# Block means of the first group issued from ScalarE, smaller pieces of v, and other places for q, w_val and k loads in a fused attention and gated-convolution kernel

## The chip, the cores and the metric

The kernel runs on one core of one Trainium2 chip. The metric is device time in microseconds (us); three runs of the kernel before gave a median of 293.86 us (293.66 to 294.35). PE is TensorE, DVE is VectorE, ACT is ScalarE, POOL is GpSimd, and SP is SyncE, which here only issues DMAs. PEld is the loading of weights into PE.

## The reference

Attention over 4 batches and 8 heads of 768 positions, 64 wide, in which each query sees a window of its neighbours and one summary of every block of 32 positions, followed by a projection, a causal convolution that makes a gate, and a second projection:

```python
k_sum = k.reshape(B, H, nb, block, D).max(axis=3)      # block 32: maximum of k
v_sum = v.reshape(B, H, nb, block, D).mean(axis=3)     # mean of v
mask_l = np.abs(pos[:, None] - pos[None, :]) < window  # window 16
scores_all = np.concatenate([scores_l_m, scores_s + log(block)], axis=-1)
a = softmax(scores_all)
x = a @ np.concatenate([v, v_sum], axis=2)             # (4, 768, 512) after a transpose
gate = sigmoid(causal_conv5(x, conv_w))
out = (gate * (x @ w_val)) @ w_out
```

All inputs are float32 except those that the kernel takes as 64-bit words and converts on the chip (w_val, w_out and the convolution weights).

## The kernel before

**Units and groups.** A unit is one pair of heads over four tiles of 64 queries; there are 48, numbered u = 0 to 47. Four units (the four pairs `pr`) make a group g = u // 4, a third of a batch. For each unit, `stage_s` multiplies q by a tile of 120 columns of k per query tile (window, own block of 64, and the 24 block maxima), DVE masks the scores and finds row minima (`sn`, `nm`), ACT takes the exponent (`p`), `stage_n` normalises on POOL, `stage_t` transposes on PE and copies to SBUF on ACT (`pt`, `pts`), and `stage_av` multiplies by v (`x`), copies the result out on ACT (`xf`, `xh`), splits it on POOL (`xl`) and makes the five convolution taps on ACT or DVE (`g`). When a group's four units are through, eight pieces of projection work are queued for PE: `val` (four, with w_val) and `out` (two, with w_out).

**Data in SBUF.** `qbd` has two buffers, one per group in turn. Each pair has two buffers of k, one per batch in turn. v has two buffers, one per group in turn: `v_g` takes the place of `v_(g-2)`, and its load has to wait until the last unit of that group (u = 4(g-2) + 3) has been multiplied. A v buffer holds, on 120 partitions, 16 rows before the tile, 64 own rows, 16 rows after, and twice 12 rows of block means. The three groups of loaded rows come by three DMAs (`load_v`, L110, of 8192 bytes a row), and the 24 rows of means by four DMAs from the small tile `vs` in SBUF (`fill_vs`, L166). In k, `prep_k` (L117) computes the block maxima (`ks`) on DVE and copies them between the loaded columns; only then can a unit of the new batch use that k. For the means of v, `prep_v` adds on POOL, or in batch 0 `prep_v0` on DVE, from a transposed copy `vT`.

**What sets the order.** SP's instructions stand in the order of the code. The other engines' orders are made by a scheduler when the kernel is built, from the same code. `LOADS` (L44) is the order of the first loads: k, q, vT of batch 0 (n), mask (m), identity (i), v of group 0, convolution weights (c), the four rows of w_val (w), and q of group 1 (Q). After them `side_work` (L451) runs once per step s (step s issues `stage_s` of unit s and `stage_av` of unit s - 4): at s = 3 it places the means of groups 0 and 1 and loads v of group 1, at s = 5 it loads w_out, at the first pair of each later group it loads the next q, at the last pair it loads the next v and places its means. `LOAD_K` and `PREP_K` (L47, L48) give, per pair, the step of a batch at which the next batch's k and vT are loaded, and at which they are prepared (first row for the first batch, second row for the others).

**Semaphores of the DMAs.** Each DMA, from whichever engine, reports its landing on one of eight semaphores, DMAHW0 to DMAHW7, taken in turn. A DMA waits on its issuing engine until the DMA eight places earlier, which had the same semaphore, has landed.

Of the kernel before, what the change touches and what calls it, by code (L numbers as in the profile page):

```python
# [17 lines left out]
B, H, S, D = 4, 8, 768, 64  # L18
DM = H * D
BLK, WIN = 32, 16  # L20
NB = S // BLK
QT = 64
NT = S // QT
NPR = H // 2
NTH = 3
TPU = NT // NTH
# [9 lines left out]
KALLOC = OFF_A + 2 * STEP * (NT // 2 + 1)  # L36
NK = 5
HALO = NK - 1
REBIAS = 2.0 ** ((127 - 1023) // 8)
LAG_N, LAG_T, LAG_AV = 1, 3, 4  # L40
PROJ_RATE = 1.015
VAL_COST, OUT_COST = 1.32, 2.6
ACT_TAP_G = 5
LOADS = "k0 q0 m k1 q1 n0 i k2 q2 n1 k3 q3 n2 n3 v0 c w0 w1 Q w2 w3"  # L44
CONVERT = {"wv": (0, 0, 1, 0), "wo": (6, 9, 6, 11)}
SPLIT = {"wv": (12, 4, 10, 5), "wo": (12, 9, 12, 12)}
LOAD_K = ((6, 7, 8, 9), (1, 2, 8, 4))  # L47
PREP_K = ((9, 10, 11, 11), (5, 8, 9, 8))  # L48
PREP_V0 = (1, 2, 3, 3)


# [1 line left out]
def tile_attention_then_gated_conv(  # L53
# [13 lines left out]
    nc = tc.nc  # L67
# [13 lines left out]
    for i in range(NQB):  # L81
        t = cpool.tile([P, NPR, SG], F32, tag=f"qbd{i}", name=f"qbd{i}")
# [13 lines left out]
    def load_q(g):  # L96
        b, th = divmod(g, NTH)
        nc.sync.dma_start(qbd[g % NQB], qT[b, th])

    def load_k(b, pr):  # L100
        t = ld.tile([P, KALLOC], F32, tag=f"k{pr}", name=f"k_{b}_{pr}")
        nc.sync.dma_start(t[:, :KTOT], kT[b, pr])
        ktile[b, pr] = t

    def load_vT(b, pr):
        t = ld.tile([P, S], F32, tag="vT", name=f"vT_{b}_{pr}")
        nc.sync.dma_start(t, vT[b, pr])
        vTt[b, pr] = t

    def load_v(g):  # L110
        b, th = divmod(g, NTH)
        t = ld.tile([KW, TPU, DM], F32, tag="v", name=f"v_{g}")
        for r0, r1, s0 in ((0, WIN, 0), (OFF_O, OFF_B, WIN), (OFF_N, KW, WIN + QT)):
            nc.sync.dma_start(t[r0:r1], vw[b, th, s0 : s0 + r1 - r0])  # L114
        vtile[g] = t

    def prep_k(b, pr):  # L117
        t = ktile[b, pr]
        ks = wk.tile([P, NB], F32, tag="ks", name=f"ks_{b}_{pr}")
        own = t[:, OFF_O : OFF_O + STEP * NT].rearrange("p (t c) -> p t c", c=STEP)[:, :, :QT]  # L120
        nc.vector.tensor_reduce(  # L121
            ks.rearrange("p (t j) -> p t j", j=2),
            own.rearrange("p t (j c) -> p t j c", c=BLK),
            AX.X,
            ALU.max,
        )
        for half, n in ((0, NT // 2 + 1), (1, NT // 2)):
            c0 = OFF_A + half * STEP
            dst = t[:, c0 : c0 + 2 * STEP * n].rearrange("p (t c) -> p t c", c=2 * STEP)[:, :, :HB]
            src = ks[:, half * HB : half * HB + HB]  # L130
            nc.vector.tensor_copy(dst, src.unsqueeze(1).broadcast_to([P, n, HB]))  # L131
# [32 lines left out]
        vsum[b] = t  # L164

    def fill_vs(g):  # L166
        b = g // NTH
        src = vsum[b]
        vr = vtile[g].rearrange("p (t e) c -> p e t c", e=2)
        for e in range(2):  # L170
            for half in range(2):
                off = OFF_A if (e == half) else OFF_B
                nc.sync.dma_start(  # L173
                    vr[off : off + HB, e],
                    src[half * HB : half * HB + HB].unsqueeze(1).broadcast_to([HB, TPU // 2, DM]),
                )
# [5 lines left out]
    def to_f32(dst, raw, n, nm, bufs):  # L182
        words = raw.rearrange("p (n two) -> p two n", two=2)
        low, high = words[:, 0], words[:, 1]
        sc = wk.tile([P, n], F32, tag=f"sc{n}", name=f"sc_{nm}", bufs=bufs)
        nc.scalar.activation(sc, high.bitcast(F32), AF.Copy, scale=REBIAS)
        hi = sc.bitcast(U32)
# [43 lines left out]
    def load_cw():  # L231
        dst = cwt.rearrange("p a k -> p (a k)")
        if not wide:
            nc.sync.dma_start(dst, cw)
            return
        raw = cpool.tile([P, 2 * NPR * NK], U32, tag="cwraw", name="cwraw")
        nc.sync.dma_start(raw, cw.bitcast(U32))
        to_f32(dst, raw, NPR * NK, "cw", 1)

    def load_w4(nm, src, ks):  # L240
# [6 lines left out]
        n=load_vT0,  # L247
        w=lambda i: load_w4("wv", wv, (i,)),
        v=load_v,
        m=lambda i: nc.sync.dma_start(mask, maskc),  # L250
        i=lambda i: nc.sync.dma_start(ident, identc),
        c=lambda i: load_cw(),
        Q=lambda i: load_q(1),
    )
    for a in LOADS.split():
        acts[a[0]](int(a[1]) if len(a) > 1 else 0)
# [6 lines left out]
    def group(g):  # L263
        if g not in grp:
# [3 lines left out]
                gt=wk.tile([P, NPR, SG], F32, tag="gt", name=f"gt_{g}"),  # L268
                xf=wk.tile([P, NPR, HALO + SG], F32, tag="xf", name=f"xf_{g}"),
            )  # L270
            halo = grp[g]["xf"][:, :, :HALO]
            if g % NTH == 0:
# [69 lines left out]
    def stage_av(u):  # L342
# [16 lines left out]
        x = G["xf"]  # L359
        c0 = HALO  # L360
        if g:
# [20 lines left out]
    def proj_val(g, co):  # L382
# [5 lines left out]
        if g == 0:  # L388
            for ci in range(4):
                nc.tensor.matmul(  # L390
                    pp[:, :SG], wvf[:, ci, cs], G["xf"][:, ci, HALO:],
                    start=(ci == 0), stop=(ci == 3),
# [62 lines left out]
    def side_work(s):  # L455
# [8 lines left out]
        if s == NPR - 1:  # L464
            prep_vs(0)
            fill_vs(0)
            load_v(1)
            fill_vs(1)
        if s == NPR + 1:
            load_w4("wo", wo, (2, 3, 0, 1))  # L470
        if s >= NPR and g + 1 < NG:
            if pr == 0:
                load_q(g + 1)
            if pr == NPR - 1:
                load_v(g + 1)
                if th + 1 < NTH:
                    fill_vs(g + 1)
        if b + 1 < B:
            for i in range(NPR):
                if w == LOAD_K[b > 0][i]:  # L480
                    load_k(b + 1, i)
                    load_vT(b + 1, i)
                if w == PREP_K[b > 0][i]:
                    prep_k(b + 1, i)
# [38 lines left out]
def _layout(q, k, v, moe_w_val, moe_conv_w, moe_w_out):  # L523
    f = np.float32
    qT = q.reshape(B, NPR, 2, NTH, SG, D).transpose(0, 3, 2, 5, 1, 4)
    qT = qT.reshape(B, NTH, 2 * D, NPR, SG)
    kt = k.reshape(B, NPR, 2, S, D).transpose(0, 1, 2, 4, 3).reshape(B, NPR, 2 * D, S)
    kT = np.zeros((B, NPR, 2 * D, KTOT), f)
    for t in range(NT):
        c = OFF_O + STEP * t  # L530
        kT[..., c : c + QT] = kt[..., t * QT : (t + 1) * QT]
    vT = v.reshape(B, NPR, 2, S, D).transpose(0, 1, 2, 4, 3).reshape(B, NPR, 2 * D, S)
    vn = np.zeros((B, S + 2 * WIN, DM), f)
    vn[:, WIN : WIN + S] = v.transpose(0, 2, 1, 3).reshape(B, S, DM)
    vw = np.zeros((B, NTH, QT + 2 * WIN, TPU, DM), f)
    for t in range(NT):
        vw[:, t // TPU, :, t % TPU] = vn[:, t * QT : t * QT + QT + 2 * WIN]
    cw = moe_conv_w.reshape(NK, NPR, 2 * D).transpose(2, 1, 0).reshape(2 * D, NPR * NK)

    def words(a):  # L540
        a = np.ascontiguousarray(a)
        return a.view(np.int64) if a.dtype == np.float64 else a

    loc = np.full(KW, -1)
    loc[:WIN] = np.arange(WIN)
    loc[OFF_O:OFF_B] = WIN + np.arange(QT)
    loc[OFF_N:] = WIN + QT + np.arange(WIN)
    qi = np.arange(2 * D)[:, None] % QT
    second = np.arange(2 * D)[:, None] >= QT
    maskc = np.zeros((2 * D, 3, KW), f)  # L550
    for mv in range(3):
        lo = np.where((mv == 0) & ~second, WIN, 0)
        hi = np.where((mv == 2) & second, WIN + QT, QT + 2 * WIN)
        ok = (loc > qi) & (loc < qi + 2 * WIN) & (loc >= lo) & (loc < hi)
        m = np.where(ok, 0.0, -1.0e9 * math.sqrt(D))
        m = np.where(loc[None, :] < 0, math.log(BLK) * math.sqrt(D), m)
        maskc[:, mv] = m
    return dict(
        qT=qT, kT=kT, vT=vT, vw=vw, wv=words(moe_w_val), cw=words(cw), wo=words(moe_w_out),
        maskc=maskc, identc=np.eye(2 * D, dtype=f),  # L560
    )
# [24 lines left out]
```

## Time and profile before

| | us |
|---|---|
| median of three runs | 293.86 |
| profiled execution, whole time | 295.11 |
| its span, first to last instruction | 293.3 |
| PE busy | 250.3 |
| DVE busy | 218.0 |
| ACT busy | 190.1 |
| POOL busy | 155.0 |

The profile's page gives the busy time per engine, then the span in 40 slices of 7.33 us with the busy share of each in tenths, then the chain of work that ended last. The other views are answers drawn from the same trace: the timeline (start, duration, engine, line, operation, out<-in, and in brackets the idle time of the engine before it and what ended it), the waits (engine and line, whom it waited for: total us, times, longest), windows (a stretch, its length, busy time of PE, PEld, DVE, ACT and POOL with counts, then granted PE clock, DMA share and GB/s), and groups of instructions (count, busy us, mean ns of one, idle before). SPq rows of a timeline show when SP issued a DMA and how long the issue took, not the transfer. The profiled execution lies 1.25 us above the median of the runs shown.

### The profile page before, as it was taken

To read this page: it belongs to the slowest core of one execution; us is meant where nothing else is said; L and a number is where in the kernel's file an instruction comes from. 1 tells how busy PE (TensorE), PEld (TensorE's weight loads), DVE (VectorE), ACT (ScalarE), POOL (GpSimd) and SP (SyncE) were. 2 spreads that over 40 slices of the span, in tenths; PEclk is the share of its full clock that TensorE was granted. 3 is DMA by queue.
4 is the path that set the end of the run, shared out by engine and by line. 5 is a ranking of instruction groups with operands and counts; after the bars stand their busy time and mean duration, and the time that the engine had idled before them with its cause. 6 is when DMAs were issued, how large, how long until landed. Compare 5 with 4: busy or idle time off the path is not lost.

```text
span 293.3 us, 7550 instructions
## 1 busy us (share of the span) xinstructions
PE 250.3 (85%) x2592; PEld 200.8 (68%) x2592; DVE 218.0 (74%) x827; ACT 190.1 (65%) x686; POOL 155.0 (53%) x224
## 2 busy tenths in 40 slices
PE   1352856999989998979989889699999999999994
PEld 0231634677767775867766677589888887989893
DVE  1948789988679857756749988587898897876420
ACT  1436868857966975947955978377695877735231
POOL 0124346998677666455467578264465453723240
PEclk9999995599999999999999999979999999999999
DMA  7999690781484283660474476706335052202011
GB/s 221 385 242 303 177 368 4 211 305 55 111 254 160 70 207 125 165 200 3 116 235 169 133 235 172 230 0 160 123 104 141 2 152 93 75 0 75 0 74 72
DMA packets 15302, 43.46 MB, mean 148 GB/s; under 512 B 2592, under 2 KB 3360, under 8 KB 14112
## 3 DMA queue, kind: packets, MB, share of 16 engines
q1 hardware_dynamic: 15264, 42.98, 47.7%
q8 instruction: 21, 0.34, 0.5%
q14 instruction: 17, 0.14, 0.2%
HBM read 34.32 MB, written 6.29 MB: 138 GB/s over the span
## 4 chain that ended last, share of the span: by engine, by line
PE 43%; DMA 22%; SPq 13%; DVE 10%; ACT 7%; issue 2%; ACTq 0%
PE val L397 15%; PE out L419 13%; DMA k<-in_kT_dram 12%; SPq L173 7%; PE x L351 7%; PE s L293 4%; PE pt L337 4%; DMA v<-in_vw_dram 3%; DMA v<-vs 3%; SPq L114 3%; DVE g L377 3%; DMA qbd<-in_qT_dram 3%; ACT p L316 3%; DVE ks L121 2%; DVE k L131 2%
## 5 line engine op out<-in xcount | busy, mean ns | idle before, releaser
L377 DVE SCALAR_TENSOR_TENSOR g<-xf,cwt,g 128x256 f32<-128x256 f32 x192 | 93.2, 486 | 7.2 <-ACT g L370 3.7
L316 ACT ACTIVATE p<-sn,nm 128x120 f32<-128x120 f32 x192 | 74.1, 391 | 27.4 <-DVE nm L305 24.3
L397 PE MATMUL val<-xh,wv 128*128 128x256 f32 x352 | 75.2, 296 | 2.2 <-ACT xh L362 1.2
L328 POOL TENSOR_TENSOR p<-p,ri 128x480 f32<-128x480 f32 x48 | 48.5, 1011 | 33.1 <-DVE ri L326 20.9
L397 PEld LDWEIGHTS val<-xh,wv 128*128 128x128 f32 x352 | 57.6, 192 | 6.2 <-ACT xh L362 2.6
L419 PE MATMUL out<-wo,gh 128*128 128x512 f32 x192 | 60.8, 402 | 1.1 <-ACT ob L425 1.1
L365 POOL TENSOR_TENSOR xl<-xf,xh 128x256 fp32r<-128x256 f32 x44 | 32.4, 737 | 41.0 <-ACT xf L363 40.9
L397 PE MATMUL val<-xl,wv 128*128 128x256 f32 x176 | 50.6, 290 | 0.0
L293 PE MATMUL s<-k,qbd 64*64 64x120 f32 x768 | 37.8, 300 | 14.9 <-DVE nm L305 6.1
L407 POOL TENSOR_TENSOR gl<-gf,gh 128x256 fp32r<-128x256 f32 x48 | 35.0, 734 | 22.6 <-ACT gh L406 22.2
L305 DVE CUSTOM_DVE_ANT_0 sn<-s,mask 128x120 f32<-128x120 f32 x192 | 43.7, 275 | 4.2 <-PE s L293 3.9
L293 PEld LDWEIGHTS s<-k,qbd 64*64 64x64 f32 x768 | 23.9, 146 | 26.4 <-issue 11.8
L351 PE MATMUL x<-pts,v 120*64 120x64 f32 x768 | 34.4, 232 | 7.5 <-DMA v<-vs 3.5
L419 PEld LDWEIGHTS out<-wo,gh 128*128 128x128 f32 x192 | 34.2, 188 | 8.4 <-ACT ob L425 1.5
L351 PEld LDWEIGHTS x<-pts,v 120*64 120x64 f32 x768 | 27.3, 140 | 18.1 <-issue 4.6
L337 PE MATMUL pt<-ident,p 128*120 128x128 f32 x192 | 33.3, 299 | 5.3 <-ACT pts L339 3.9
L316 ACT ACTIVATION_READ_ACCUMULATOR p<-sn,nm 128x1 f32 x192 | 37.2, 194 | 0.0
L419 PE MATMUL out<-wo,gl 128*128 128x512 f32 x96 | 37.1, 400 | 0.0
L142 POOL TENSOR_TENSOR vT<-vT 128x384 f32<-128x384 f32 (+3 forms) x48 | 27.4, 577 | 18.1 <-DMA vT<-in_vT_dram 16.7
L397 PEld LDWEIGHTS val<-xl,wv 128*128 128x128 f32 x176 | 33.8, 192 | 1.0 <-issue 0.5
L380 ACT ACTIVATE gt<-g 128x256 f32<-128x256 f32 x48 | 18.7, 389 | 22.4 <-DVE g L377 22.1
L405 DVE SCALAR_TENSOR_TENSOR gf<-gt,val 128x256 f32<-128x256 f32 x48 | 19.7, 417 | 15.3 <-PE val L397 13.1
(44 smaller groups left out, 300.8 us busy)
## 6 DMA issues: line engine op xcount, KB each, us to landing
k<-in_kT_dram SPq DMA_DIRECT2D x16, 478.0 KB
vT<-in_vT_dram SPq DMA_DIRECT2D x16, 384.0 KB
v<-in_vw_dram SPq DMA_DIRECT2D x12, 512.0 KB
out_dram<-ob SPq DMA_DIRECT2D x24, 256.0 KB
qbd<-in_qT_dram SPq DMA_DIRECT2D x11, 512.0 KB
v<-in_vw_dram SPq DMA_DIRECT2D x24, 128.0 KB
v<-vs SPq DMA_DIRECT2D x48, 48.0 KB
raw_wv<-in_wv_dram SPq DMA_DIRECT2D x4, 512.0 KB
```

The lines of the kernel that those rows point to most:

```text
L142: nc.gpsimd.tensor_tensor(dst, src[:, :, :n], src[:, :, n : 2 * n], ALU.add)
L293: nc.tensor.matmul(sp[64 * e : 64 * e + 64, h, j * KW : j * KW + KW], qbd[g % NQB][64 * h : 64 * h + 64, pr, i * QT : i * QT + QT], ktile[ ...
L305: nc.vector.tensor_tensor_reduce(sn[:, n, :], sp[:, h, j * KW : j * KW + KW], mask[:, mv, :], -1.0 / math.sqrt(D), 3.0e38, ALU.add, ALU.mi ...
L316: nc.scalar.activation(p[:, n, :], sn[:, n, :], AF.Exp, bias=nm[:, n : n + 1], scale=-1.0, accum_out=rs[:, n : n + 1],)
L328: nc.gpsimd.tensor_tensor(pn, s["p"], ri.unsqueeze(2).broadcast_to([P, TPU, KW]), ALU.mult)
L337: nc.tensor.transpose(pt[:KW, i, :], s["pn"][:, i, :], ident)
L351: nc.tensor.matmul(xp[h * D : (h + 1) * D, i * QT : (i + 1) * QT], v[:, i, c0 : c0 + D], s["pts"][:, 2 * (i // 2) + h, (i % 2) * QT : (i % ...
L365: nc.gpsimd.tensor_tensor(G["xl"][:, pr, :], x[:, pr, c0 : c0 + SG], G["xh"][:, pr, :].bitcast(F32), ALU.subtract)
L377: nc.vector.scalar_tensor_tensor(gt, x[:, pr, o : o + SG], cwt[:, pr, k : k + 1], gt, ALU.mult, ALU.add)
L397: nc.tensor.matmul(pp[:, :SG], w[:, ci, cs], G[x][:, ci, :], start=(n == 0), stop=(n == 11))
L407: nc.gpsimd.tensor_tensor(G["gl"][:, co, :], gf, G["gh"][:, co, :].bitcast(F32), ALU.subtract)
L419: nc.tensor.matmul(pp, G[gx][:, ci, si * P : si * P + P], w[:, ci, :], start=(n == 0), stop=(n == 11))
```

## The change

The four DMAs that place the means of group 0 are issued by ACT instead of SP (later groups stay on SP). v lies in DRAM as two halves of two tiles each, so that each row of a v load is two pieces of 4096 bytes instead of one of 8192. In the first loads, the last two rows of w_val come before q of group 1. `LOAD_K` and `PREP_K` have other steps.

```diff
+VP = TPU // 2
-LOADS = "k0 q0 m k1 q1 n0 i k2 q2 n1 k3 q3 n2 n3 v0 c w0 w1 Q w2 w3"
+LOADS = "k0 q0 m k1 q1 n0 i k2 q2 n1 k3 q3 n2 n3 v0 c w0 w1 w2 w3 Q"
-LOAD_K = ((6, 7, 8, 9), (1, 2, 8, 4))
-PREP_K = ((9, 10, 11, 11), (5, 8, 9, 8))
+LOAD_K = ((5, 6, 8, 9), (1, 2, 5, 6))
+PREP_K = ((7, 8, 10, 11), (4, 5, 8, 9))
@@ load_v
-            nc.sync.dma_start(t[r0:r1], vw[b, th, s0 : s0 + r1 - r0])
+            src = vw[b, th, :, s0 : s0 + r1 - r0].rearrange("e r t c -> r e t c")
+            nc.sync.dma_start(t[r0:r1].rearrange("r (e t) c -> r e t c", e=VP), src)
@@ fill_vs
+        eng = nc.sync if g else nc.scalar
-                nc.sync.dma_start(
+                eng.dma_start(
@@ _layout
-    vw = np.zeros((B, NTH, QT + 2 * WIN, TPU, DM), f)
+    vw = np.zeros((B, NTH, VP, QT + 2 * WIN, 2, DM), f)
-        vw[:, t // TPU, :, t % TPU] = vn[:, t * QT : t * QT + QT + 2 * WIN]
+        i = t % TPU
+        vw[:, t // TPU, i // 2, :, i % 2] = vn[:, t * QT : t * QT + QT + 2 * WIN]
```

Three places show what this does to the order of instructions. The first is on ACT, near the start: `vs_0` are the means, `sc_cw` and `sc_wv0..3` the first step of converting the weights, `p_3` the exponents of unit 3, `pts_1` the copy of unit 1's transposed weights. In brackets stands what a row waits for. Before:

```order
L339 COPY pts_0_285<-pt_0_280 120x512 [waits PE_49]
L186 ACTIVATE sc_cw_117<-cwraw_115 128x20 [waits DMAHW1_49]
L186 ACTIVATE sc_wv0_137<-raw_wv0_122 128x512 [waits DMAHW2_49]
L316 ACTIVATE p_3_289,rs_3_291<-sn_3_288,nm_3_290 128x120 [waits DVE_49] x3
L339 COPY pts_1_343<-pt_1_338 120x512 [waits PE_49]
L186 ACTIVATE sc_wv1_142<-raw_wv1_124 128x512 [waits DMAHW3_49]
```

And now:

```order
L342 COPY pts_0_285<-pt_0_280 120x512 [waits PE_49]
L189 ACTIVATE sc_cw_117<-cwraw_115 128x20 [waits DMAHW1_49]
L176 DMA v_0_111<-vs_0_262 12x2x512 [waits DMAHW2_49,Activation_49]
L176 DMA v_0_111<-vs_0_262 12x2x512 [waits DMAHW4_49]
L189 ACTIVATE sc_wv0_137<-raw_wv0_122 128x512
L176 DMA v_0_111<-vs_0_262 12x2x512 [waits DMAHW6_49]
L189 ACTIVATE sc_wv1_142<-raw_wv1_124 128x512 [waits DMAHW3_49]
L176 DMA v_0_111<-vs_0_262 12x2x512 [waits DMAHW0_49]
L319 ACTIVATE p_3_289,rs_3_291<-sn_3_288,nm_3_290 128x120 [waits DVE_49] x4
L342 COPY pts_1_343<-pt_1_338 120x512 [waits PE_49]
```

Four DMAs with waits of their own have moved in ahead of `p_3` and `pts_1`. Counted through the eight semaphores, they wait for the landing of the first row of w_val, of the third, of q of group 1, and of the middle piece of v of group 1.

The second place is on SP, where k of batch 3 is loaded (`k_3_2` is batch 3, pair 2; `v_8` the v of group 8). Before:

```order
L98 DMA qbd0_81<-in_qT_dram 128x1024
L102 DMA k_3_3_2224<-in_kT_dram 128x956
L107 DMA vT_3_3_2226<-in_vT_dram 128x768
L426 DMA out_0_dram<-ob_3_1_2241 128x512
L114 DMA v_8_2474<-in_vw_dram 16x2048
L114 DMA v_8_2474<-in_vw_dram 64x2048
L114 DMA v_8_2474<-in_vw_dram 16x2048
L173 DMA v_8_2474<-vs_2_1823 12x2x512 x4
L98 DMA qbd1_82<-in_qT_dram 128x1024
L102 DMA k_3_2_2564<-in_kT_dram 128x956
```

And now:

```order
L99 DMA qbd0_81<-in_qT_dram 128x1024
L429 DMA out_0_dram<-ob_3_1_2247 128x512
L103 DMA k_3_2_2319<-in_kT_dram 128x956
L108 DMA vT_3_2_2321<-in_vT_dram 128x768
L103 DMA k_3_3_2396<-in_kT_dram 128x956
L108 DMA vT_3_3_2398<-in_vT_dram 128x768
L116 DMA v_8_2488<-in_vw_dram 16x2x1024
L116 DMA v_8_2488<-in_vw_dram 64x2x1024
L116 DMA v_8_2488<-in_vw_dram 16x2x1024
L176 DMA v_8_2488<-vs_2_1823 12x2x512 x4
L99 DMA qbd1_82<-in_qT_dram 128x1024
```

`k_3_2` has moved from behind the load of v of group 8 to ahead of it, one group earlier; it now stands behind the load of v of group 7 (just above these rows). In batch 1 the same holds of `k_2_2`, which moves from behind v of group 5 to behind v of group 4, and of `k_1_1`, which moves ahead of v of group 2.

The third place is on PE, where unit 16 takes the q that was loaded behind v of group 3. That v could be loaded once x of unit 7 was done; x of unit 8 follows a little later. Before, these rows come next after x of unit 8 and the piece `val_1_3`:

```order
L419 MATMUL out_1_0_1283<-wo_87,gh_1_1077 128x512 x2
L419 MATMUL out_1_0_1283<-wo_87,gl_1_1078 128x512
L419 MATMUL out_1_0_1283<-wo_87,gh_1_1077 128x512 x2
L419 MATMUL out_1_0_1283<-wo_87,gl_1_1078 128x512
L293 MATMUL s_16_1306<-k_1_0_431,qbd0_81 64x120 x8
L419 MATMUL out_1_1_1363<-wo_87,gh_1_1077 128x512 x2
```

Now x of unit 9 and nearly all of `out_1_0` and `out_1_1` come first, and s of unit 16 stands here:

```order
L422 MATMUL out_1_0_1289<-wo_87,gl_1_1078 128x512
L340 MATMUL pt_13_1305<-ident_84,p_13_1038 120x128 x3
L354 MATMUL x_10_1087<-pts_10_1034,v_2_503 64x64 x8
L340 MATMUL pt_13_1305<-ident_84,p_13_1038 120x128
L296 MATMUL s_16_1312<-k_1_0_377,qbd0_81 64x120 x8
```

So between x of unit 7 and s of unit 16 there was one x, and there are now three (units 8, 9 and 10), with 22 of the 24 matmuls of `out` for group 1 in place of 6.

## Prediction

> **What bounds the kernel now.** I read the page first: busy times, the PE line of the slices, and the chain of work that ended last with its shares.
>
> ```profile
> span 293.3 us, 7550 instructions
> PE 250.3 (85%) x2592; PEld 200.8 (68%) x2592; DVE 218.0 (74%) x827; ACT 190.1 (65%) x686; POOL 155.0 (53%) x224
> PE   1352856999989998979989889699999999999994
> PE 43%; DMA 22%; SPq 13%; DVE 10%; ACT 7%; issue 2%; ACTq 0%
> ```
>
> PE is busiest, but carries only 43% of the chain; DMAs and their issue on SP carry 35%. The slices say where: the last third is solid PE, the first fifth (to about 45 us) is thin, and single dips stand between. So time is to be had in the front and at the gates, not in the last 95 us. Next, the waits of SP and DVE (engine, line, releaser: us, times, longest), and the chain (start, us, what):
>
> ```profile
> SPq L114 <- PE x L351: 116.5, 10, 16.8
> DVE ks L121 <- DMA k<-in_kT_dram: 16.5, 9, 4.0
> 21.13 9.10 DMA v<-vs
> 181.84 6.01 DMA k<-in_kT_dram
> ```
>
> SP waits ten times, 116.5 us in all, for the last x of an old group before it may load v. Everything behind that load in SP's order starts late: the fills, the next q and any k placed there. DVE then waits 16.5 us for k in nine places. This is the loop that the change works on.
>
> **The front (F).** Here are SP's DMAs from 16 to 33 us in before (start, us of issue, line), then ACT's, PE's and two window rows (busy and count per engine, clock, DMA share, GB/s).
>
> ```profile
> 20.10 3.47 SPq L173 DMA_DIRECT2D v<-vs  x4
> 24.84 0.59 SPq L114 DMA_DIRECT2D v<-in_vw_dram  x1
> 29.76 0.83 SPq L173 DMA_DIRECT2D v<-vs  x1
> 32.29 0.80 SPq L173 DMA_DIRECT2D v<-vs  x1
> 22.87 0.38 ACT L316 ACTIVATE p<-sn,nm 128x120 f32<-128x120 f32 x1
> 32.68 0.37 ACT L363 COPY xf<-x 128x256 f32<-128x256 f32 x1
> 30.27 0.48 PE L351 MATMUL x<-pts,v 120*64 120x64 f32 x4 [3.48 <-DMA v<-vs]
> 15.00:20.00 5.00, 2.64 (x22) 1.64 (x22) 2.46 (x12) 2.20 (x10) 0.99 (x1) 1.00 0.99 197
> 20.00:25.00 5.00, 1.38 (x6) 1.03 (x7) 3.24 (x16) 3.29 (x11) 0.99 (x1) 1.00 1.01 397
> ```
>
> A DMA waits on its issuing engine until the one eight earlier has landed, so issue times on SP are also landing times: the v load of group 1 left at 24.84, when q of group 1 landed, and the last fill at 32.29, when the middle piece of that load landed. Now the four fills of group 0 stand in ACT's order, and wait there for the first and third rows of w_val, for q of group 1 and for that middle piece. That q is now behind two more rows of w_val: 27.4 us is my estimate, from 24.84 plus the two rows (256 KB each) at the 197 GB/s of 15 to 20 us. The middle piece follows the q by some 3.5 us: the same piece of group 0 landed at 20.10, about 3.5 us after vT ahead of it. That makes 30.9, and after 0.83 of issue ACT is free at 31.7. In before it took `p_3` at 22.87.
>
> What stands behind the last fill on ACT is shown by its groups between 0 and 60 us (us of all, mean ns | idle before).
>
> ```profile
> L339 ACT COPY pts<-pt 120x512 f32<-120x512 f32 x7 | 4.0, 572 | 0.0
> L186 ACT ACTIVATE sc_wv<-raw_wv 128x512 f32<-128x512 f32 x4 | 2.6, 666 | 2.0 <-DMA raw_wv<-in_wv_dram 2.0
> L228 ACT CAST wv<-wvf 128x512 fp32r<-128x512 f32 x4 | 2.5, 618 | 1.7 <-DVE wvf L193 1.7
> 30.00:40.00 10.00, 7.79 (x81) 5.82 (x82) 8.06 (x24) 8.10 (x27) 4.50 (x5) 1.00 0.74 244
> ```
>
> Ahead of `xf_0` ACT has eight exponents of 0.38 (`p_3`, `p_4`: 3.0), two `pts` (1.1), two casts (1.2) and two first steps (1.3), 6.7 us, and I add 0.7 for a wait on DVE's part of the conversion: 31.7 + 7.4 = 39.1, where before has 32.68, or 6.4 later. Not all of it reaches the end: DVE, which feeds every later group, was busy 8.06 of the 10 us from 30 to 40, and makes up the 1.9 us it had idle. **F = +4.5.** Bounds: if the pieces of v stream at 397 instead of 197 GB/s, each of the two v loads (768 KB) takes 2.0 instead of 4.0 us, ACT is free 4 us earlier and more work fits into holes: −1.5. If the middle piece lands only at 32.29, as before, ACT is 1.4 later, and k of batch 1, pair 1, whose preparation (0.95 + 2 × 0.49, rows below) now comes early, is ahead of it on DVE: 4.5 + 1.4 + 1.9, about +8.
>
> What makes room is SP: the 3.47 us of issue leave it. In a sentence of its own: the Trainium skill, "DMA: Bandwidth & Descriptors", section "Issuing engines are not separate DMA queues", says that transfers of all issuers share the same 16 engines, so that a second issuer saves only the time of issuing; the DMA share of 0.99 and 1.01 above agrees. By it nothing lands sooner, and ACT would pay the issue and no more; that outcome is the first rival.
>
> **Smaller pieces (V).** The issue of a later group, then one where SP itself waited:
>
> ```profile
> 50.65 1.59 SPq L114 DMA_DIRECT2D v<-in_vw_dram  x3
> 162.25 2.33 SPq L114 DMA_DIRECT2D v<-in_vw_dram  x3
> 164.62 3.31 SPq L173 DMA_DIRECT2D v<-vs  x4
> ```
>
> Three plain v pieces cost SP 1.59; a fill with the same three-dimensional form as the new pieces costs up to 3.31 / 4 = 0.83, so three could cost 2.3 to 2.5. Three groups are gated by q right behind v: I take a third of 0.9 × 3, **V = +0.9**, halfway to the old cost for each (bounds 0 and +2.2).
>
> **The gates (X).** These rows show PE and DVE where k or q came last, and the grouped cost of preparing k; the bracket is the idle time and its releaser.
>
> ```profile
> 86.36 0.64 PE L293 MATMUL s<-k,qbd 64*64 64x120 f32 x16 [1.45 <-DMA qbd<-in_qT_dram]
> 110.70 0.95 DVE L121 TENSOR_REDUCE ks<-k 128x24 f32<-128x768 f32 x1 [2.50 <-DMA k<-in_kT_dram]
> 128.87 0.95 DVE L121 TENSOR_REDUCE ks<-k 128x24 f32<-128x768 f32 x1 [2.95 <-DMA k<-in_kT_dram]
> 187.87 0.95 DVE L121 TENSOR_REDUCE ks<-k 128x24 f32<-128x768 f32 x1 [3.06 <-DMA k<-in_kT_dram]
> 173.19 0.95 DVE L121 TENSOR_REDUCE ks<-k 128x24 f32<-128x768 f32 x1
> L131 DVE COPY k<-ks 128x84 f32<-128x84 f32 (+1 forms) x32 | 14.3, 488 | 0.1
> 125.00:135.00 10.00, 8.47 (x83) 6.57 (x84) 6.37 (x25) 5.09 (x22) 6.31 (x10) 1.00 0.43 141
> 165.00:175.00 10.00, 8.48 (x123) 7.11 (x122) 8.73 (x43) 8.22 (x34) 7.05 (x9) 1.00 0.80 246
> 185.00:190.00 5.00, 2.87 (x41) 1.94 (x39) 2.13 (x4) 0.74 (x3) 0.86 (x1) 1.00 0.84 255
> 190.00:195.00 5.00, 4.77 (x38) 4.70 (x39) 4.53 (x16) 3.79 (x15) 3.86 (x8) 0.66 0.00 0
> ```
>
> - *Group 4, s of unit 16 (86.36).* It waited 1.45 for q behind v of group 3. PE now has two more x and 16 more matmuls of `out` to do first, more than 1.45 us of work: **−1.4** (bounds −1.4 and 0).
> - *Batch 2 (110.70).* `k_2_2` now stands where `k_2_3` stood, behind the load of v of group 4 with a q and an output. DVE comes to it about as early: the 2.50 stay, **0** (−1 to +2).
> - *Group 6 (128.87).* No k is left behind v of group 5, so 2.95 goes; q of group 6 stands behind that v and is late next, but PE's idle time here is only 10 − 8.47 = 1.5, and the DVE slack (3.6) covers the rest. **−2.0** (−3.0 to 0).
> - *Group 8 (173.19).* `k_3_2` and `k_3_3` were there in time; now `k_3_2` stands behind v of group 7, q and an output. At before's pace DVE reaches its row near 169, and the load, issued at 168.60 plus the 6.01 of the chain's k, lands near 174: 5 us on DVE. Against it, PE now has three x units and projections ahead of s of unit 32 instead of two, and its own idle time here, 1.5, goes. I take **+0.5**, nearer to that 1.5 of idle PE than to the stall (−1.5 to +4).
> - *Group 9 (187.87).* `k_3_2` was the last late one: 3.06 on DVE, after which PE idles 2.1 of 5 us, and then runs 5 us at a granted clock of 0.66, worth 0.34 × 4.77 = 1.6. Without a k behind v of group 8 the next late is q, in time by PE's stock of work. 3.06 + 1.6, less what q may keep: **−4.0** (−4.8 to −2).
>
> The w_val rows that now land before q of group 1 are within F. The k of batch 1, pair 1, ahead of v of group 2, is prepared early in DVE's idle 1.9, which F has spent; its price is in F's upper bound.
>
> **Sum:** +4.5 + 0.9 − 1.4 + 0 − 2.0 + 0.5 − 4.0 = **−1.5**. The profiled execution took 295.11 in all (293.3 of span and 1.8 around it), so 293.6; it lay 1.25 above the median, so against the 293.86 of the runs it is **292.4**.
>
> **Rivals.**
> - *ACT pays only the issue.* If q and the pieces of v land early enough, the fills cost ACT 3.47 us in a time in which it was idle anyway for DVE's minima. For it speaks that ACT was busy only 3.29 of 5 us from 20 to 25; against it that wire time stood at 1.01 there. F is then about +0.5, the sum −5.5, the time 288.4.
> - *ACT held longer: slower.* The middle piece of v of group 1 lands after 32.4 instead of 30.9. For it: that is where it lands in before, by the row at 32.29, and two rows of w_val are now ahead of it. F = 8, sum +2.0, time 295.9. The case decides from F above 6.0, where the sum becomes zero.
> - *The wait for `k_3_2` comes in full: slower.* DVE stands at the row of unit 32's k for 5 us, all of DVE's later work with it, and PE's stock (two x) runs out. Then group 8 costs +4.5 instead of +0.5: sum +2.5, time 296.4. Against it: the 3.06 at 187.87 drained PE only because just one unit was left to it.
> - *The waits move but do not go.* q of groups 6 and 9 stands behind the same v and takes over what k held. If group 6 gives 0.5 instead of 2.0, the sum is 0.0 and the time 293.9.
>
> **How the numbers follow.** The forecast (−5 to −0.7) has .34, ACT's issue alone .18, ACT held longer .22, `k_3_2` in full .13, waits that only move .13. Faster by over 0.2% (0.6 us, about what a measurement of this kernel can tell from no change) is .34 + .18 = .52; within it .13; slower .22 + .13 = .35. The range: low 286.0, the first rival with group 6 and 9 at their bounds (−1.0 and −0.8) and half a microsecond of F; high 298.5, the third rival with F 2 us over its value. About 2 in 10 lie outside.
>
> **What would show it.** In the profile after: ACT's four rows of `v<-vs` between 20 and 32 us, the last ending near 31.7 (before 28: first rival; after 32.4: second); `xf_0` near 39; s of unit 16 without a wait for q; DVE's reduce for k near 110 still waiting some 2.5, that near 129 not, a new wait of up to 5 near 170, none at 188, and no stretch at 0.66 behind it. Three v pieces on SP show V: 1.6 or 2.4. The forecast is wrong if F leaves −1.5 to +8, or if a gate that I call relieved shows a wait of the same length for q.

## The result, and the profile after

The changed kernel is slower: a median of 309.65 us (306.95 to 311.0, four runs) against 293.76 for the kernel before in the same session, a ratio of 1.053 with a 95% interval of 1.046 to 1.061. The forecast was 292.4, with a range up to 298.5: wrong in sign and outside the range. Executions of one kernel differ by some 3%: a time below is the median of all executions of a run, and a ratio compares only those within 1.5% of each kernel's fastest, so that the two need not agree to the last microsecond. The changed kernel's profiled execution took 310.01 us with a span of 308.2, 14.9 more than the 293.3 of before.

From the page after, the lines that answer to those of before (instructions and span, busy times, PE in 40 slices, the clock in the same slices, the chain by engine):

```profile
span 308.2 us, 7561 instructions
PE 252.8 (82%) x2592; PEld 202.0 (66%) x2592; DVE 218.2 (71%) x827; ACT 190.7 (62%) x686; POOL 153.8 (50%) x224
PE   1340475399999798799979997899999999999994
PEclk9999999759999999989997999799999999999999
PE 38%; DMA 24%; DVE 18%; ACT 7%; SPq 4%; POOL 4%; issue 3%; ACTq 0%; POOLq 0%; DVEq 0%
```

PE runs the same 2592 matmuls. The new hole is in the slices from the fourth to the eighth, 23 to 62 us: 0 and 4 stand there first, where before had 2 and 8. The clock dips in the two slices from 54 to 69 us and, a little, at three later places (in tenths of full speed), and PE's busy time is 2.5 us longer, 252.8 against 250.3.

Where the time went is seen by a cut through both traces. First the kernel before, then after: busy time and count of each engine from 0 to 70 us, and from 70 to 200.

```profile
0.00:70.00 70.00, 43.54 (x403) 30.38 (x403) 54.72 (x198) 41.94 (x146) 34.45 (x44) 0.90 0.75 238
70.00:200.00 130.00, 117.57 (x1314) 94.49 (x1312) 98.68 (x401) 93.94 (x353) 80.57 (x126) 0.99 0.50 149
```

```profile
0.00:70.00 70.00, 31.30 (x317) 21.95 (x318) 49.63 (x173) 35.43 (x125) 26.74 (x34) 0.93 0.66 204
70.00:200.00 130.00, 117.51 (x1253) 93.01 (x1253) 94.50 (x381) 89.95 (x336) 81.16 (x128) 0.96 0.53 164
```

By 70 us PE has been busy for 43.54 us before and for 31.30 after: 12.24 us more idle time. From 70 to 200 it is busy for 117.57 and 117.51, the same. So the front loses 12.2, and the gates, where the prediction had its 6.9 us of gain, take no idle time away. With the 2.5 of longer busy time that is 14.7 of the 14.9. The longer busy time is seen in the second stretch: PE does 1253 matmuls there instead of 1314 in the same time, at a mean granted clock of 0.96 instead of 0.99.

Next, ACT in the trace after, from 20 us on (start, us, what; the bracket is the idle time ahead of it and its releaser), with what stands between left out. An ACTq row shows when ACT issued a DMA, and does not count as busy, so that the brackets on the rows behind hold the time at the fills too, under the name of whatever else that row needed:

```profile
21.54 3.29 ACTq L176 DMA_DIRECT2D v<-vs  x2
24.88 0.66 ACT L189 ACTIVATE sc_wv<-raw_wv 128x512 f32<-128x512 f32 x1 [4.18 <-DMA raw_wv<-in_wv_dram]
28.02 0.79 ACTq L176 DMA_DIRECT2D v<-vs  x1
28.86 0.66 ACT L189 ACTIVATE sc_wv<-raw_wv 128x512 f32<-128x512 f32 x1 [3.31 <-DMA qbd<-in_qT_dram]
31.27 0.79 ACTq L176 DMA_DIRECT2D v<-vs  x1
32.11 0.39 ACT L319 ACTIVATE p<-sn,nm 128x120 f32<-128x120 f32 x1 [2.59 <-DVE wvf L196]
...
41.83 0.35 ACT L366 COPY xf<-x 128x256 f32<-128x256 f32 x1
```

The third fill leaves when q of group 1 has landed, the fourth at 31.27. Between 21 and 32 us ACT computes 1.3 us; `p_3` starts at 32.11 instead of 22.87, and `xf_0` at 41.83 instead of 32.68. The same place on PE, the first row from the kernel before, the others from after:

```profile
24.70 1.08 PE L337 MATMUL pt<-ident,p 128*120 128x128 f32 x4 [3.12 <-ACT pts L339]
34.34 1.08 PE L340 MATMUL pt<-ident,p 128*120 128x128 f32 x4 [12.65 <-ACT pts L342]
...
58.40 1.08 PE L296 MATMUL s<-k,qbd 64*64 64x120 f32 x16 [2.90 <-issue]
62.23 1.08 PE L296 MATMUL s<-k,qbd 64*64 64x120 f32 x16 [2.75 <-DVE nm L308]
63.24 1.12 PE L354 MATMUL x<-pts,v 120*64 120x64 f32 x16
```

PE stands 12.65 us for one copy on ACT, where it stood 3.12. The last three rows show a second place: x of unit 3, which lets SP load v of group 2 (at 64.40 instead of 50.65), stands behind s of units 8 and 9 on PE, and PE is idle for 2.90 us (the profile shows nothing that it waited for: "issue") and 2.75 us ahead of these two. In the order of before only s of unit 8 stood ahead of it.

SP is held too: its load of w_out waits for ACT in the third row, and the first k of batch 1, behind it, is loaded at 40.92 instead of 35.61. The late k cost nothing by itself, as DVE's first reduce for batch 1, at 50.29, shows no wait.

### The profile page after: what moved, and what is told of

It reads as the page before. It is cut to its first block, busy times and chain, and to the rows that moved or that the text cites. A ratio compares the mean times of both kernels' runs of the same rounds, so it can differ in the third digit from the quotient of the medians.

```text
span 308.2 us, 7561 instructions
## 1 busy us (share of the span) xinstructions
PE 252.8 (82%) x2592; PEld 202.0 (66%) x2592; DVE 218.2 (71%) x827; ACT 190.7 (62%) x686; POOL 153.8 (50%) x224
## 2 busy tenths in 40 slices
DMA packets 16454, 43.46 MB, mean 141 GB/s; under 512 B 2592, under 2 KB 3360, under 8 KB 16416
## 4 chain that ended last, share of the span: by engine, by line
PE 38%; DMA 24%; DVE 18%; ACT 7%; SPq 4%; POOL 4%; issue 3%; ACTq 0%; POOLq 0%; DVEq 0%
PE out L422 13%; PE val L400 12%; DMA k<-in_kT_dram 8%; DMA vT<-in_vT_dram 6%; PE x L354 5%; DVE g L380 5%; DMA v<-vs 5%; PE pt L340 4%; ACT p L319 4%; PE s L296 3%; DMA raw_wv<-in_wv_dram 3%; DVE sn L308 3%; DVE k L133 3%; DVE ks L123 2%; SPq L176 2%
## 5 line engine op out<-in xcount | busy, mean ns | idle before, releaser
L331 POOL TENSOR_TENSOR p<-p,ri 128x480 f32<-128x480 f32 x48 | 47.4, 987 | 66.1 <-DVE ri L329 26.2
L400 PE MATMUL val<-xh,wv 128*128 128x256 f32 x352 | 72.6, 294 | 5.6 <-ACT ob L428 3.0
L296 PE MATMUL s<-k,qbd 64*64 64x120 f32 x768 | 38.7, 304 | 18.4 <-DVE nm L308 10.1
L400 PE MATMUL val<-xl,wv 128*128 128x256 f32 x176 | 51.8, 295 | 0.0
L340 PE MATMUL pt<-ident,p 128*120 128x128 f32 x192 | 34.0, 301 | 18.2 <-ACT pts L342 17.5
L368 POOL TENSOR_TENSOR xl<-xf,xh 128x256 fp32r<-128x256 f32 x44 | 32.4, 735 | 32.6 <-ACT xf L366 32.6
L410 POOL TENSOR_TENSOR gl<-gf,gh 128x256 fp32r<-128x256 f32 x48 | 34.9, 735 | 27.4 <-ACT gh L409 23.3
L296 PEld LDWEIGHTS s<-k,qbd 64*64 64x64 f32 x768 | 24.6, 148 | 29.7 <-issue 20.7
L319 ACT ACTIVATION_READ_ACCUMULATOR p<-sn,nm 128x1 f32 x192 | 38.3, 199 | 0.0
L340 PEld LDWEIGHTS pt<-ident,p 128*120 128x120 f32 x192 | 22.4, 147 | 23.2 <-issue 14.3
L144 POOL TENSOR_TENSOR vT<-vT 128x384 f32<-128x384 f32 (+3 forms) x48 | 27.4, 583 | 8.8 <-DMA vT<-in_vT_dram 8.3
L409 ACT CAST gh<-gf 128x256 fp32r<-128x256 f32 x48 | 19.2, 415 | 18.7 <-DVE gf L408 18.4
```

The lines of the kernel that those rows point to most:

```text
L144: nc.gpsimd.tensor_tensor(dst, src[:, :, :n], src[:, :, n : 2 * n], ALU.add)
L296: nc.tensor.matmul(sp[64 * e : 64 * e + 64, h, j * KW : j * KW + KW], qbd[g % NQB][64 * h : 64 * h + 64, pr, i * QT : i * QT + QT], ktile[ ...
L319: nc.scalar.activation(p[:, n, :], sn[:, n, :], AF.Exp, bias=nm[:, n : n + 1], scale=-1.0, accum_out=rs[:, n : n + 1],)
L331: nc.gpsimd.tensor_tensor(pn, s["p"], ri.unsqueeze(2).broadcast_to([P, TPU, KW]), ALU.mult)
L340: nc.tensor.transpose(pt[:KW, i, :], s["pn"][:, i, :], ident)
L368: nc.gpsimd.tensor_tensor(G["xl"][:, pr, :], x[:, pr, c0 : c0 + SG], G["xh"][:, pr, :].bitcast(F32), ALU.subtract)
```

## The experiments

Each run's ratio is to the kernel before on the same chip. The kernel that an edit starts from is named in its expectation.

**1. ACT's fills alone.**

```diff
+        eng = nc.sync if g else nc.scalar
-                nc.sync.dma_start(
+                eng.dma_start(
```

> The kernel before, with one edit: the four fills of group 0 are issued by ACT. Theory (the hold of ACT is the whole loss: ACT stands at its own DMAs until 32 us, PE has no transposed weights, DVE no exponents and no sc_wv, and the front moves by some 13 us): 304 to 310 us, v of group 2 loaded on SP near 63 us instead of 50.65. Rival (the k loads moved forward, with their preparation on DVE between 50 and 60 us, make most of the 14 us): 296 to 299 us, the 4.5 us forecast for the front.

307.94 us, 1.048 (1.037 to 1.059): the one edit makes the whole loss. v of group 2 is loaded at 60.87 us. The rival, the early k, falls: this run leaves k where it was.

**2. Everything but ACT's fills.**

```diff
-        eng = nc.sync if g else nc.scalar
-                eng.dma_start(
+                nc.sync.dma_start(
```

> The changed kernel with the four fills of group 0 back on SP; pieces of v, order of the first loads and places of k as changed. Theory (only ACT's hold costs; the gates give little): 291 to 296 us, v of group 2 loaded by 52 us. Rival (the early k costs DVE, and late k costs at groups 5 and 8): 299 to 306 us, v of group 2 loaded at 56 us or later.

295.64 us, 1.0066 (1.0027 to 1.0106), at the upper edge of the theory's range; v of group 2 is loaded at 54.32, later than the 52 that the theory allowed. Put back on SP, the fills give 14.0 of the 15.9 us; the other three edits together cost about 2.

**3. The order of the first loads alone.**

```diff
-... v0 c w0 w1 Q w2 w3"
+... v0 c w0 w1 w2 w3 Q"
```

> The kernel before, with one edit: the third and fourth rows of w_val loaded ahead of q of group 1. Theory: nothing that waits for that q is near in the front, 293 to 295 us. Rival (that q, and behind it v of group 1, comes later and holds unit 4 and the second fills): 296 to 300 us.

298.35 us, 1.020 (1.012 to 1.027): a miss, the rival's range. PE in that run, where s of unit 4 needs the q that now comes last:

```profile
27.92 1.08 PE L293 MATMUL s<-k,qbd 64*64 64x120 f32 x16 [2.77 <-DMA qbd<-in_qT_dram]
```

Here PE waits 2.77 for that q. The profile names the wait; that it makes all of the 4.7 us (298.35 against 293.65) isn't shown.

**4. The places of k alone.**

```diff
-LOAD_K = ((6, 7, 8, 9), (1, 2, 8, 4))
-PREP_K = ((9, 10, 11, 11), (5, 8, 9, 8))
+LOAD_K = ((5, 6, 8, 9), (1, 2, 5, 6))
+PREP_K = ((7, 8, 10, 11), (4, 5, 8, 9))
```

> The kernel before, with one edit: the steps at which k and vT of batches 1 to 3 are loaded and prepared. Theory (the gates win a little and lose as much, as the prediction's terms X without F: -6.9 us at the most): 287 to 294 us, without DVE's waits of 2.95 and 3.06 us near groups 6 and 9. Rival (k of the third and fourth pair behind v of groups 4 and 7 stops DVE): 296 to 300 us, with a new stop of 4 us or more on PE near 165 us.

292.03 us, 0.997 (0.9935 to 1.0003): at most a small gain. DVE's waits for k do shrink, from 16.5 us to

```profile
DVE ks L121 <- DMA k<-in_kT_dram: 8.9, 6, 4.0
```

so 7.6 us less of waiting on DVE brought 1.6 us, or nothing. PE's own idle time (span less busy time) is 2.0 us shorter, 41.0 against 43.0: most of DVE's waiting had not been idle time of PE.

**5. The pieces of v alone,** with the layout of v in DRAM as in the change, not shown again.

```diff
-            nc.sync.dma_start(t[r0:r1], vw[b, th, s0 : s0 + r1 - r0])
+            src = vw[b, th, :, s0 : s0 + r1 - r0].rearrange("e r t c -> r e t c")
+            nc.sync.dma_start(t[r0:r1].rearrange("r (e t) c -> r e t c", e=VP), src)
```

> The kernel before, with one edit: v in two halves of 4096 bytes for each row. Theory (the pieces cost SP little more issue and no engine waits on it in the front): 292 to 295 us, with the three v pieces at 1.6 to 1.8 us of issue on SP. Rival (the smaller pieces carry some of what the kernel without ACT's fills lost, 2 us beside the k loads' gain): 296 to 298 us.

293.82 us, 1.000 (0.993 to 1.008): nothing that can be measured; the interval leaves room for 2 us either way. The four parts don't add up exactly (3, 4 and 5 by their ratios give about +5, together in run 2 they cost 2), since each edit also moves the orders of the engines.

**6. The same fills from POOL.** This takes away ACT's hold, but leaves the fills outside SP.

```diff
-        eng = nc.sync if g else nc.scalar
+        eng = nc.sync if g else nc.gpsimd
```

> The changed kernel, its four fills of group 0 issued by POOL instead of ACT. In the order that stands there, POOL's fills wait for the means alone and for no landing of another transfer. Theory (what costs is ACT standing at a landing, not that the fills leave SP or land at another time): p of unit 3 on ACT by 24 us and 291 to 297 us, as with the fills on SP. Rival (fills outside SP's queue land late or slow the loads beside them, whoever issues them): 300 us or more, with x of unit 0 after 34 us.

298.65 us, 1.015 (1.007 to 1.024). ACT is free (its first exponent of unit 3 starts at 21.76), and 11 of the 15.9 us are gone; but the time lies 1.6 above the theory's range, below the rival's, with single executions from 293.67 to 300.38. The trace is that of the slowest, 300.38. POOL's row in it, and a row on PE:

```profile
19.12 2.44 POOL L176 DMA_DIRECT2D v<-vs  x4 [2.36 <-ACT vs L165]
```

```profile
30.42 1.08 PE L296 MATMUL s<-k,qbd 64*64 64x120 f32 x16 [5.74 <-DMA qbd<-in_qT_dram]
```

The fills are issued at once, with no wait for another landing; in the trace they report on four semaphores of their own, so the rule of the eight holds here for SP's and ACT's DMAs, not for POOL's. What makes the rest is open. PE waits 5.74 for q of group 1, as in run 3, but its idle time over all is 44.3 us, the same as in run 7 below, and the rest stands in its busy time, 254.3 against 246.9, at a mean granted clock of 0.960 against 0.975. Nor is it certain that there is a rest: the intervals of run 2 (to 1.0106) and of this run (from 1.0068) overlap.

**7. Two of the four fills on ACT.** This tells the wait from the issue.

```diff
-                eng.dma_start(
+                (nc.sync if e else eng).dma_start(
```

> The changed kernel with two of the four fills of group 0 on ACT and two on SP. Counted through the eight semaphores, ACT's two then wait for transfers that have long landed (pieces of v of group 0 and ahead of it), so that ACT pays the issue alone, about 1.7 us. Theory (the wait costs, not the issue): 293 to 298 us, p of unit 3 on ACT by 26 us. Rival (issuing from ACT costs in proportion: half of 14): 301 to 304 us.

293.52 us, 1.0046 (1.000 to 1.009). ACT around its two DMAs:

```profile
21.24 2.40 ACTq L176 DMA_DIRECT2D v<-vs  x2
23.69 0.66 ACT L189 ACTIVATE sc_wv<-raw_wv 128x512 f32<-128x512 f32 x1 [2.29 <-DMA v<-vs]
24.25 0.38 ACT L319 ACTIVATE p<-sn,nm 128x120 f32<-128x120 f32 x1
```

ACT is in `p_3` at 24.25 instead of 32.11. Half of the DMAs cost not half of the loss but next to none of it: the price lies in the waits, not in the issue. PE's idle time is 44.3 us, against 55.4 in the changed kernel. The rest of the kernel stays as changed, the late q of group 1 too.

**8. x of unit 3 earlier on PE.**

```diff
-        head = {mybir.EngineType.PE} if s < NPR else set()
+        head = {mybir.EngineType.PE} if s < NPR or s == NPR + 3 else set()
```

> The changed kernel with one more edit: at the step of unit 7 PE's work is taken in the code's order. ACT's rows up to its copy of x of unit 0 stay word for word, so ACT is held until 32 us as before the edit, but x of unit 3 now stands ahead of s of units 7, 8 and 9 on PE. Theory (9 us of the loss are the hold itself, the other 4 to 5 come because x of unit 3 stands behind s of units 8 and 9, which wait for DVE): v of group 2 loaded near 58 us instead of 64.4, and 302 to 307 us. Rival (the whole loss is fixed by the hold): no change, 308 to 311 us.

303.9 us, 1.026 (1.011 to 1.040), in the theory's range, from four executions between 299.97 and 310.13. v of group 2 is loaded at 57.12 instead of 64.40, with ACT held as long (its last fill leaves at 30.24). But that the place of x of unit 3 was part of the loss isn't shown. From the page of this run:

```profile
span 300.0 us, 7560 instructions
PE 244.5 (81%) x2592; PEld 199.2 (66%) x2592; DVE 217.5 (72%) x827; ACT 188.3 (63%) x686; POOL 154.4 (51%) x224
```

PE is idle for 55.5 us here and for 55.4 in the changed kernel. What is shorter is its busy time, 244.5 against 252.8, at a mean granted clock of 0.992 against 0.965. The edit moves PE's other work of that step too: s of units 7 to 9 come later than in the changed kernel.

**9 and 10. k ahead of v,** once on the kernel before with the changed places of k, and once on the whole changed kernel:

```diff
-LOAD_K = ((5, 6, 8, 9), (1, 2, 5, 6))
+LOAD_K = ((5, 6, 6, 6), (1, 2, 2, 2))
+LOAD_T = ((5, 6, 8, 9), (1, 2, 5, 6))
...
                     load_k(b + 1, i)
-                    load_vT(b + 1, i)
+                if w == LOAD_T[b > 0][i]:
+                    load_vT(b + 1, i)
```

> The kernel before with the changed places of k (as in the run with those alone), and k of the third and fourth pair of each next batch loaded two or three steps earlier still, ahead of the v that SP waits for; vT stays. Theory (in the changed kernel the waits for k only moved, because k of the third pair still stands behind a v): DVE waits for k fall from 8.9 us (that run) to under 6, none of them after 100 us, 286 to 291 us. Rival (q behind the same v holds the groups anyway): 291 to 294 us.

295.47 us, 1.014 (1.006 to 1.022): a miss, slower than both. DVE's waits for k in that run, the longest of them, and DVE from 40 to 60 us:

```profile
DVE ks L122 <- DMA k<-in_kT_dram: 12.9, 5, 5.5
95.25 0.95 DVE L122 TENSOR_REDUCE ks<-k 128x24 f32<-128x768 f32 x1 [5.51 <-DMA k<-in_kT_dram]
40.00:50.00 10.00, 6.37 (x76) 4.48 (x75) 10.00 (x31) 8.17 (x27) 6.59 (x8) 0.83 0.75 304
50.00:60.00 10.00, 5.77 (x33) 4.39 (x34) 10.00 (x29) 4.15 (x13) 6.63 (x11) 0.75 0.76 229
```

The theory had the waits at under 6 us; they are 12.9, against 8.9 in run 4. For batch 1, where k comes early, DVE's order takes all four reduces between 44.17 and 56.15 us, in a stretch in which DVE is busy throughout. For batch 2 all four k are loaded between 87.98 and 91.8 us, and DVE stands 5.51 us for the first of them. Which of the two makes the run slower was not tested; a full DVE in the front is not enough for it, since in run 11, the fastest of all, the four reduces stand as early (42.77 to 53.10).

> The changed kernel whole, with k of the third and fourth pair loaded ahead of v in the same way. Theory (the 14 us of the front stay, but the later waits for k, 20.2 us on DVE, of which 2.2 stood near 120 us and 3.7 near 186, go in part): 301 to 307 us, DVE's waits for k under 12 us. Rival (the front alone sets the end, the waits for k cost nothing): 308 to 311 us.

302.29 us, 1.038 (1.030 to 1.047): 7.4 less than the changed kernel, in the theory's range, with

```profile
DVE ks L124 <- DMA k<-in_kT_dram: 10.5, 4, 4.0
```

in place of 20.2. But PE's idle time is only 1.7 us shorter (53.7 against 55.4); most of the gain in the profiled execution is busy time of PE, 245.1 against 252.8, at a mean granted clock of 0.988 against 0.965. The same edit loses on one kernel and wins on the other.

**11 and 12. Towards a faster version:** the edit of run 8 on run 9's kernel, and on run 4's.

> The run with k ahead of v on the kernel before, with PE's work at the step of unit 7 in the code's order too (x of unit 3 ahead of s of units 7 and 8). Theory (v of group 2 is loaded when x of unit 3 is done, so it comes 2 to 6 us earlier and group 4's q with it): 284 to 289 us. Rival (x of unit 3 takes the place of s, so that DVE is starved between 30 and 45 us): 291 us or more.

289.27 us, 0.992 (0.987 to 0.997; one execution of 347.36 lies outside all others): faster than both kernels, than the one before by under 1%, and just above the expected range. v of group 2 is loaded at 44.98 instead of 50.65.

> The kernel before with the changed places of k (all fills on SP, first loads and v as before) and PE's work at the step of unit 7 in the code's order; k of the third and fourth pair is not loaded ahead of v. Theory (x of unit 3 ahead of s of units 7 and 8 lets v of group 2 load near 45 us instead of 48 to 51, and the early k's preparation on a full DVE, which the run with k ahead of v paid, is gone): 285 to 289 us, at or below the run that has both. Rival (k ahead of v was what won there): 290 to 293 us.

295.26 us, 1.017 (1.006 to 1.029): a miss. The ratio rests on three executions of the kernel before; the median of all eleven, 293.84, is only 1.4 lower. So neither part wins alone (run 9 without the earlier x, this run without the earlier k, neither faster than the kernel before); only both together do. Why wasn't found out.

**All runs side by side.** PE's idle time, the span less the busy time on each page (one execution of each kernel), sorts them: 53.7 to 55.5 us in the four that have all four fills on ACT (the changed kernel, runs 1, 8 and 10), 41.0 to 45.3 in all others, 43.0 in the kernel before and 42.6 in run 2. What the other edits did lies within these bands, and in part in PE's busy time, which goes from 244.5 to 255.0 us for the same matmuls.

## Why the prediction was wrong

**F, the front: the mechanism was right, its price was not.** The working had ACT free at 31.7 and bound to the landings of the first and third row of w_val, of q and of the middle piece of v; ACT's first row behind the fills is at 32.11. That it came so near is in part luck. The q was put at 27.4 and landed by 28.02, but each row of w_val is 512 KB, as the row below from the kernel before says, and not 256; and the stretch from 20 to 30 us moved 310 GB/s, not 197. The two errors cancel.

```profile
raw_wv<-in_wv_dram SPq DMA_DIRECT2D x4, 512.0 KB
```

Runs 1, 2 and 7 show that this wait, and not the issue, is the loss. But the term was +4.5 (at most 8), and it measured 12 to 14 (12.24 us of PE's time by 70 us; 14.0 between run 2 and the changed kernel). The step that failed is the one from `xf_0` to the end: "Not all of it reaches the end: DVE ... makes up the 1.9 us it had idle." Three things were wrong with it.

- The row for `xf_0` itself was forecast at 39.1 and came at 41.83, because more of DVE's pieces of the weights now stand ahead of its minima for unit 4 (39.92, with s of unit 4 done on PE by 36.43), on which the exponents ahead of `xf_0` wait. ACT's cast in between waits 2.59 us for DVE, where 0.7 was allowed.
- The credit went the wrong way. With ACT held, DVE gets neither exponents' sums nor converted words, and idles more, not less. From 20 to 30 us, before and then after:

```profile
20.00:30.00 10.00, 3.17 (x24) 2.11 (x24) 6.87 (x29) 5.58 (x17) 4.88 (x4) 1.00 0.99 310
```

```profile
20.00:30.00 10.00, 1.08 (x4) 0.70 (x4) 3.75 (x17) 2.00 (x5) 0.98 (x1) 1.00 1.03 310
```

DVE falls from 6.87 to 3.75 us, and that work is then to be done later. From 50 to 60 us DVE is full, 10.00 against 9.30, and PE is idle for 5.55 us instead of 1.16 (first row before, the other two after; that the work put off is what fills DVE there is argued, not shown):

```profile
50.00:60.00 10.00, 8.84 (x53) 6.27 (x51) 9.30 (x35) 7.06 (x25) 9.17 (x10) 0.59 0.70 200
50.00:60.00 10.00, 4.45 (x58) 3.09 (x58) 10.00 (x33) 6.05 (x22) 6.90 (x12) 0.91 0.00 0
60.00:70.00 10.00, 7.77 (x79) 6.00 (x80) 8.22 (x41) 7.33 (x31) 6.56 (x7) 0.58 0.36 94
```

- What was counted was a lag on ACT at one instruction. What reaches the end is the time in which PE stood idle. From 70 to 200 us PE is idle for 12.4 us in both kernels, so there was room to make it up, but nothing was made up; after 200 us it is solid in both. Between `xf_0` and x of unit 3 the lag grows from 9.15 us to 13.75 (the v loads at 50.65 and 64.40), since s of units 8 and 9 stand ahead of that x. That order could be read before the run, and the working didn't look at it. What it cost stays open, since run 8, which moves it, leaves PE's idle time as it was.

**The first loads** were put "within F". Alone they cost 4.7 us (run 3): q of group 1 is needed by s of unit 4 at 28 us. This was a term of its own, and was left out; beside ACT's hold it adds little, as run 1 has the whole loss without it.

**V, the pieces:** +0.9 was forecast, at 2.3 to 2.5 us of issue as one bound; SP in the trace after has

```profile
64.40 1.68 SPq L116 DMA_DIRECT2D v<-in_vw_dram  x3
```

1.68 against 1.59, so the issue was nearer to the lower bound. Run 5 shows no effect, but cannot tell 0.9 us from nothing.

**X, the gates,** is the second term that failed, by somewhat less than F. The sum of -6.9 was read wait by wait, and most of the waits went or stayed as forecast; but their price on PE was not there: run 4, with the places of k alone, won 1.6 us or nothing, and in the changed kernel PE's idle time from 70 to 200 us is what it was. Group 4's wait for q is gone: no row of PE in the waits of the trace after names a DMA. The reduces for k after 110 us:

```profile
120.59 0.95 DVE L123 TENSOR_REDUCE ks<-k 128x24 f32<-128x768 f32 x1 [2.17 <-DMA k<-in_kT_dram]
124.83 0.92 DVE L123 TENSOR_REDUCE ks<-k 128x24 f32<-128x768 f32 x1
165.70 0.95 DVE L123 TENSOR_REDUCE ks<-k 128x24 f32<-128x768 f32 x1 [1.52 <-DMA k<-in_kT_dram]
169.70 0.95 DVE L123 TENSOR_REDUCE ks<-k 128x24 f32<-128x768 f32 x1
186.02 0.95 DVE L123 TENSOR_REDUCE ks<-k 128x24 f32<-128x768 f32 x1 [3.67 <-DMA k<-in_kT_dram]
189.02 0.95 DVE L123 TENSOR_REDUCE ks<-k 128x24 f32<-128x768 f32 x1
```

The 2.50 of batch 2 stays (2.17), and the two late waits of 2.95 and 3.06, behind v of groups 5 and 8, are gone. The new one for `k_3_2`, forecast at up to 5, is there with 3.67 (the row at 186.02); that is the wait of the third rival, and group 8 pays for it as group 9 did before:

```profile
190.00:200.00 10.00, 8.14 (x82) 6.01 (x77) 8.81 (x34) 6.60 (x27) 8.94 (x17) 0.83 0.74 201
```

PE idles 1.9 us and then runs part of the stretch at a lower clock, mean 0.83. Over all, DVE's waits for k grew from 16.5 us; the largest new ones, of 2.67 us at 74.36, 1.21 at 78.25 and 2.25 at 100.14, stand where the prediction had none:

```profile
DVE ks L123 <- DMA k<-in_kT_dram: 20.2, 9, 3.8
```

So the fourth rival's mechanism (the waits move but do not go) holds for k itself, not for q. What these waits cost is open: with 10.5 in place of 20.2 us run 10 is 7.4 us faster, but PE's idle time in its trace only 1.7 us shorter; in run 4 a wait taken from DVE was worth a fifth of its length, or nothing.

**The rivals.** The slower one with ACT held longer had the right place and sign. Its condition (the middle piece landing after 32.4) wasn't met, nor needed: the wait as forecast was enough, at three times its price. What spoke for it was misread: the last three fills of group 1 in the kernel before are issued back to back (30.63 to 33.09), so that the one at 32.29 waited for nothing, and counted through the eight semaphores it needs the third fill of group 0, not that piece. The first rival (ACT pays the issue only) was no case of this kernel, but is what run 7 made. The Trainium skill's sentence behind it ("DMA: Bandwidth & Descriptors", "Issuing engines are not separate DMA queues": another issuer saves only the time of issuing) agrees with run 7, where nothing is won by it. The loss of this kernel was not in the issue, but in what the issuer had to wait for.

## What to carry to other kernels

A DMA that is handed to a computing engine brings its waits with it: find out which landing each one waits for, and what stands behind it on that engine; two that wait for nothing late cost next to none (run 7), four of which two wait for late landings cost 14 us. Price a hold in the front by the idle time of the engine that sets the end, PE here, and not by a lag at one instruction or by a wait of another engine, and read the new order up to the instruction that opens the next gate, not only up to the first row that is late. When two runs differ, split the difference into idle and busy time of that engine, with the granted clock beside it, before naming an edit as the cause: runs 8 and 10 were faster than the changed kernel mostly in busy time.

## What the runs showed of the hardware that wasn't expected

The same four DMAs took SP 3.47 us to issue in the kernel before, and POOL 2.44 us in run 6, where they waited for no other transfer. In the changed kernel they spread over 10.5 us on ACT (21.54 to 32.06). PE's busy time for the same 2592 matmuls went from 244.5 us at a mean granted clock of 0.992 (run 8) to 255.0 at 0.960 (run 2), but not strictly by the mean clock: it is 247.0 at 0.958 in run 11.
